# Attention weights times values in 64x64 pieces, and the scores of eight heads in one run

## The chip, the cores and the metric

The kernel runs on one core of a Trainium2 chip. The metric is the time of one execution on the device, in microseconds; the time of a version is the median of its runs. Below, PE is TensorE (its weight loads are counted apart, as PEld), DVE is VectorE, ACT is ScalarE, POOL is GpSimd and SP is SyncE, which issues nearly all transfers.

## What is computed

Four sequences of 768 positions, eight heads of 64 features. Attention with a distance bias, over a window of 96 keys back and 8 global keys, and then a channel mix on the result, in which each position is mixed with the one before it.

```python
keep = is_global | is_local          # pos < 8, or 0 <= rel < 96
bias = -slopes * dist
a = softmax(where(keep, q @ k.T / 8 + bias, -1e9))
x = (a @ v)                          # (4, 768, 512)
xk = mu_k * x + (1 - mu_k) * x_prev;  xr = mu_r * x + (1 - mu_r) * x_prev
k = maximum(xk @ w_k, 0)             # 512 -> 1024
out = sigmoid(xr @ w_r) * (k * k @ w_v)
```

All of it is float32. The products of the channel mix are made of three matmuls each on operands split into a high and a low part.

## The kernel before

**Tiles and steps.** The 3072 rows are 24 tiles of 128 queries, six to a sequence. A loop of 25 steps handles tile n's scores in step n (`scores`, `softmax`), and tile n-2's product with v in step n (`weighted`). A step has four parts, `hp` 0 to 3. Two tiles make a chunk of the channel mix (`ffn`, `channel_mix`), a generator of 40 pieces that the loop draws on after every part, 20 pieces a step; so two steps do one chunk: 16 pieces of `kp` (x times w_k, six matmuls of 256 columns each), 8 of `z` (three matmuls of 512 columns) and 16 of `vps` (three of 512). The mix runs about one step behind the x that it reads. One step of a pair therefore holds `kp` and `z` matmuls, the other the rest of `z`, all of `vps` and the beginning of the next `kp`.

**Tiles 6 and on** (`HEAD` = 6) take another way than the first six, and the change is in this way only.

- *Scores.* A key tile `kr` holds, for each half of 64 queries, the 8 global keys and the 160 before and in the half: 168 columns. Heads 0 to 3 lie in partitions 0 to 63 and heads 4 to 7 in 64 to 127, and each half of queries is a matmul of 64 rows (features) and 64 columns (queries) (L327). The first tile of a sequence (t = 0: tiles 6, 12 and 18) has no keys before it: 128 columns, one matmul of 64 rows and 128 columns a head. Four heads are scored in part 0 and four in part 2, into the two banks of `ps_s`.
- *Softmax.* For each head DVE adds the bias and takes the minimum (L369), ACT takes the exponential and its sum (L370), DVE the reciprocal of four sums (L381, L382), and POOL scales (L385).
- *Turning.* DVE transposes the weights in blocks of 32x32 (`turn`, L393 and L394), in part 2 for the first four heads and in part 0 of the next step for the other four. SP writes the blocks to DRAM (`send`, L404) and reads them back as 128 keys by 128 queries (`receive`, L416) into `landed`, which has two kinds of blocks: kind 0 for the keys of the tile before, kind 1 for the tile's own.
- *Product with v.* For each head two matmuls of 128 rows (keys) and 64 columns (features), over 128 queries: one on the v tile before, whose first 32 rows are overwritten with global keys (`global_v`, L280), one on the own v tile (L462). Queries that do not see a block of keys meet zeros in `landed`. Tiles with t = 0 have only the second. All heads go to the one bank of `ps_a`, and ACT copies it to x (L470).

**PSUM** has eight banks: two in `ps_s`, one in `ps_a`, five in `ps_f`, which turn around among `kp`, `z` and `vps` of the mix.

**What sets the order.** Each engine works its instructions off in the order in which they were built, and waits there for semaphores. The framework arranges that order by a timeline of its own, so the order on an engine is not that of the program text alone. A float32 matmul on unsplit operands stands once in the built order and twice in the trace.

The product with v, before:

```python
for u in range(2):
    o = s["av"][64 * u : 64 * u + 64, hp * 128 : (hp + 1) * 128]
    for k, vt in enumerate(blocks):
        c = 32 * (HH * (hp % 2) + 2 * (hp // 2) + u)
        g = landed[:, :, k + 2 - nb, c : c + 32]
        pe.matmul(o, vt[:, h * 64 : (h + 1) * 64], g, start=k == 0, stop=k == nb - 1)
```

## Time and profile before

| | |
|---|---|
| median of 3 runs | 479.29 us (478.5 to 482.03) |
| the profiled execution's own time | 479.75 us |
| its span, first to last instruction | 478.0 us |
| mean granted clock of TensorE | 0.989 |
| busy, share of the span | PE 97%, PEld 81%, DVE 65%, ACT 56%, POOL 39% |

Busy is the time in which an engine had at least one instruction in work. Matmuls are pipelined, so a busy PE may still do little per microsecond: what it does is read from the starts of its instructions.

### The profile page before, as it was taken

What the parts mean: (1) busy time and instruction counts of PE and PEld (TensorE: products, weight loads), DVE (VectorE), ACT (ScalarE), POOL (GpSimd) and SP (SyncE); (2) the same over time, 40 slices, a digit from 0 to 9 for tenths busy, and PEclk for the clock granted to TensorE, in tenths of its full rate; (3) what the DMA queues carried; (4) which work ended last, traced back from release to release, by engine and by line L of the source; (5) the groups of instructions that cost most, each with busy time, mean ns of one, the idle gap of its engine ahead of it and who ended that gap; (6) DMA issues with size and microseconds to landing.
All of it is one profiled execution on the core that took longest, in us unless ns stands there. A gap on an engine that the chain in (4) does not pass through costs nothing.

```text
span 478.0 us, 10000 instructions
## 1 busy us (share of the span) xinstructions
PE 463.4 (97%) x3506; PEld 386.1 (81%) x3506; DVE 311.0 (65%) x892; ACT 266.0 (56%) x644; POOL 188.0 (39%) x357
## 2 busy tenths in 40 slices
PE   7787999999999999999999999999999999999996
PEld 6666865688798898898797897897897897898985
DVE  6788979996757757646567666666567666546221
ACT  5876654536747648547548467466549458343220
POOL 7555687733423514414225415414315325303000
PEclk9987999999999999999999999999999999999999
DMA  5998530314476575567476575477476556140001
GB/s 174 290 262 287 175 149 27 78 62 110 128 192 159 170 190 156 167 185 195 120 188 164 156 216 148 126 196 197 99 200 163 155 165 159 51 135 22 23 2 49
DMA packets 64376, 70.37 MB, mean 147 GB/s; under 512 B 8032, under 2 KB 51296, under 8 KB 64320
## 3 DMA queue, kind: packets, MB, share of 16 engines
q1 hardware_dynamic: 64176, 69.66, 53.1%
q8 instruction: 30, 0.49, 0.5%
q14 instruction: 26, 0.21, 0.1%
q10 hardware_dynamic: 144, 0.00, 0.0%
HBM read 48.99 MB, written 19.66 MB: 144 GB/s over the span
## 4 chain that ended last, share of the span: by engine, by line
PE 77%; DVE 7%; POOL 1%; issue 0%; ACT 0%; DVEq 0%; ACTq 0%
PE vps L502 9%; PE kp L502 9%; PE vps L503 9%; PE vps L504 8%; PE kp L504 8%; PE kp L503 8%; PE av L462 7%; PE s L327 5%; PE z L502 5%; PE z L503 4%; PE z L504 4%; DVE wv_lo L193 1%; DVE wk_lo L193 1%; POOL wv_hi L218 1%; DVE room L369 1%; DVE wr_lo L193 1%
## 5 line engine op out<-in xcount | busy, mean ns | idle before, releaser
L385 POOL TENSOR_SCALAR room<-room,r 128x168 f32<-128x168 f32 (+2 forms) x160 | 79.7, 516 | 161.0 <-ACT kk L539 93.2
L370 ACT ACTIVATE room<-room,nmax 128x168 f32<-128x168 f32 (+2 forms) x192 | 83.3, 435 | 44.7 <-DVE nmax L369 44.6
L502 PE MATMUL kp<-xk_hi,wk_hi 128*128 128x256 f32 x352 | 101.0, 287 | 0.7 <-DVE kk L543 0.7
L504 PE MATMUL kp<-xk_hi,wk_lo 128*128 128x256 f32 x352 | 98.7, 280 | 0.0
L503 PE MATMUL kp<-xk_lo,wk_hi 128*128 128x256 f32 x352 | 98.4, 280 | 0.0
L502 PE MATMUL vps<-wv_hi,kk_hi 128*128 128x512 f32 (+1 forms) x184 | 72.1, 392 | 0.0
L503 PE MATMUL vps<-wv_lo,kk_hi 128*128 128x512 f32 (+1 forms) x184 | 71.2, 387 | 0.0
L502 PEld LDWEIGHTS kp<-xk_hi,wk_hi 128*128 128x128 f32 x352 | 66.9, 190 | 5.3 <-issue 3.3
L504 PE MATMUL vps<-wv_hi,kk_lo 128*128 128x512 f32 (+1 forms) x184 | 70.6, 384 | 0.0
L503 PEld LDWEIGHTS kp<-xk_lo,wk_hi 128*128 128x128 f32 x352 | 66.0, 188 | 0.7 <-DVE nmax L369 0.2
L504 PEld LDWEIGHTS kp<-xk_hi,wk_lo 128*128 128x128 f32 x352 | 66.1, 188 | 0.0
L544 ACT CAST kk_hi<-kk 128x512 fp32r<-128x512 f32 x44 | 27.3, 620 | 49.5 <-DVE kk L543 49.5
L545 DVE TENSOR_TENSOR kk_lo<-kk,kk_hi 128x512 fp32r<-128x512 f32 x44 | 31.4, 713 | 21.2 <-ACT kk_hi L544 21.2
L480 DVE SCALAR_TENSOR_TENSOR mix_k<-x,mus,mix_k 128x256 f32<-128x256 f32 x44 | 27.5, 663 | 25.9 <-POOL mix_k L479 25.9
L502 PEld LDWEIGHTS vps<-wv_hi,kk_hi 128*128 128x128 f32 x184 | 34.6, 188 | 9.6 <-issue 2.1
L479 POOL TENSOR_SCALAR mix_k<-x,mus 128x256 f32<-128x256 f32 x44 | 22.9, 538 | 45.8 <-ACT x L470 45.8
L504 PEld LDWEIGHTS vps<-wv_hi,kk_lo 128*128 128x128 f32 x184 | 34.5, 188 | 7.8
L503 PEld LDWEIGHTS vps<-wv_lo,kk_hi 128*128 128x128 f32 x184 | 34.6, 188 | 6.8
L462 PE MATMUL av<-room,va 128*64 128x128 f32 x608 | 39.3, 277 | 0.0
L539 ACT ACTIVATE kk<-kp 128x512 f32<-128x512 f32 x48 | 28.2, 587 | 17.6 <-PE kp L504 13.6
L462 PEld LDWEIGHTS av<-room,va 128*64 128x64 f32 x608 | 33.9, 136 | 5.0 <-issue 2.6
L543 DVE TENSOR_TENSOR kk<-kp,kk 128x512 f32<-128x512 f32 x44 | 30.0, 683 | 11.2 <-ACT kk L539 9.4
(119 smaller groups left out, 884.7 us busy)
## 6 DMA issues: line engine op xcount, KB each, us to landing
moved<-room SPq DMA_DIRECT2D x60, 192.0 KB
k<-in_k_rows_dram SPq DMA_DIRECT2D x60, 160.0 KB
room<-moved SPq DMA_DIRECT2D x30, 256.0 KB
out_dram<-sig SPq DMA_DIRECT2D x23, 256.0 KB
va<-in_v_dram SPq DMA_DIRECT2D x21, 256.0 KB
q<-in_qT_dram SPq DMA_DIRECT2D x36, 128.0 KB
w<-in_w_k_dram SPq DMA_DIRECT2D x8, 512.0 KB
w<-in_w_v_dram SPq DMA_DIRECT2D x8, 512.0 KB
```

The costliest lines, as they stand in the source:

```text
L327: pe.matmul(ps[i][q, u * 256 : u * 256 + w], s["qr"][o : o + 64, h, q], keys, start=True, stop=True)
L370: act.activation(e[:, :w], e[:, :w], AF.Exp, bias=s["nmax"][:, h : h + 1], scale=-1.0, accum_out=s["sum"][:, h : h + 1])
L385: pool.tensor_scalar(e[:, :w], e[:, :w], r[:, i : i + 1], 1.0, op0=ALU.mult, op1=ALU.mult)
L462: pe.matmul(o, vt[:, h * 64 : (h + 1) * 64], g, start=k == 0, stop=k == nb - 1)
L480: vec.scalar_tensor_tensor(tmp[:, j, :], xc[:, j, :], m[:, j : j + 1], tmp[:, j, :], op0=ALU.mult, op1=ALU.add)
L502: pe.matmul(o, sh, mh, start=first, stop=False)
L503: pe.matmul(o, sh, ml, start=False, stop=False)
L504: pe.matmul(o, sl, mh, start=False, stop=last)
L539: act.activation(kk, pv, AF.Relu)
L543: vec.tensor_mul(kk, pv, kk)
L544: act.copy(kkh[:, 2 * fp : 2 * fp + 2, :], kk)
L545: vec.tensor_sub(kkl[:, 2 * fp : 2 * fp + 2, :], kk, kkh[:, 2 * fp : 2 * fp + 2, :])
```

## The change

The product with v of tiles 6 and on is cut into pieces of 64 keys by 64 features. Rows 0 to 63 of the keys go to the old bank (`av`), rows 64 to 127 to a second one, taken from `ps_f` (`av2`); after ACT's copy of `av` to x, DVE adds `av2` to it (L483 of the changed kernel). The blocks in `landed` are laid out anew, so that of the two kinds of key blocks one is seen by all 128 queries and the other by 64 of them: per head and half of rows there is one matmul over 128 queries and one over 64. The keys before the tile come from a tile of their own, `vb` (96 rows of v and the 32 global rows), which SP loads into `room[:, 7]` for each tile with t > 0; before, only the 32 rows were written into the old v tile.

All eight heads of a tile are scored in part 0, the first four into two banks of `ps_f`, the other four into `ps_s`. `turn` follows in parts 2 and 3 of the same step, `send` in part 3, and `receive` in part 0 of the next step.

```diff
--- before.py
+++ after.py
@@ -277,7 +277,9 @@
         b, t = divmod(n, NT)
         if n >= HEAD:
             if t:
-                nc.sync.dma_start(state[n - 1]["va"][0:32], vg)
+                vb = state[n]["vb"] = room[:, 7]
+                nc.sync.dma_start(vb[0:BACK], v[b, t * 128 - BACK : t * 128])
+                nc.sync.dma_start(vb[BACK:128], vg)
                 return
             for hh in range(HH):
                 heads = slice(HH * (hh // 2) + hh % 2, HH * (hh // 2) + hh % 2 + 3, 2)
@@ -315,9 +317,9 @@
             p = patw if t else pat0
         if n >= HEAD:
             ps = {}
-            for j in (hp // 2,):
+            for j in range(2):
                 for i in (j, j + 2):
-                    ps[i] = ps_s.tile([128, 512], F32, name=f"s_{n}_{i}", tag="s")
+                    ps[i] = (ps_s if j else ps_f).tile([128, 512], F32, name=f"s_{n}_{i}", tag="s" if j else "f")
                 for u in range(2):
                     h = 2 * j + u
                     for half in (0, 1) if t else (None,):
@@ -325,7 +327,7 @@
                         for o, i in ((0, j), (64, j + 2)):
                             keys = s["kr"][o : o + 64, h, 1, WIN - 128 : WIN] if half is None else s["kr"][o : o + 64, h, half]
                             pe.matmul(ps[i][q, u * 256 : u * 256 + w], s["qr"][o : o + 64, h, q], keys, start=True, stop=True)
-            rounds = [(j, [(i, ps[i]) for i in (j, j + 2)])]
+            rounds = [(j, [(i, ps[i]) for i in (j, j + 2)]) for j in range(2)]
         elif n < PADDED:
             ps = ps_s.tile([128, 512], F32, name=f"s_{n}_{hp}", tag="s")
             for u in range(2):
@@ -390,26 +392,23 @@
         e = room[:, 8 + 2 * j : 10 + 2 * j].rearrange("p a (u x) -> p (a u) x", u=2)
         out = turned[:, :, 128 * j : 128 * j + 128].rearrange("p l (h i) -> p h l i", h=HH)
         if n % NT:
-            vec.transpose(out[:, :, 0], e[:, :, 0:GMAX].rearrange("p (r h) k -> p r h k", r=1).to_broadcast([128, 4, HH, GMAX]))
-            vec.transpose(out[:, :, 1:6], e[:, :, GMAX:WIN].rearrange("p h (l c) -> p h l c", l=5))
-        else:
-            vec.transpose(out[:, :, 2:6], e[:, :, 0:128].rearrange("p h (l c) -> p h l c", l=4))
+            vec.transpose(out[:, :, 5], e[:, :, 0:GMAX].rearrange("p (r h) k -> p r h k", r=1).to_broadcast([128, 4, HH, GMAX]))
+            vec.transpose(out[:, :, 0:5], e[:, :, GMAX:WIN].rearrange("p h (l c) -> p h l c", l=5))
+        else:
+            vec.transpose(out[:, :, 0:4], e[:, :, 0:128].rearrange("p h (l c) -> p h l c", l=4))
 
     def send(n):
         if n < HEAD:
             return
-        l0 = 0 if n % NT else 2
+        nl = 6 if n % NT else 4
         moved = state[n]["moved"] = d_pool.tile([4, 6, 32, 256], F32, name=f"moved_{n}", tag="moved")
         for a in range(4):
-            nc.sync.dma_start(moved[a].rearrange("l q x -> q l x")[:, l0:6], turned[32 * a : 32 * a + 32, l0:6])
+            nc.sync.dma_start(moved[a].rearrange("l q x -> q l x")[:, 0:nl], turned[32 * a : 32 * a + 32, 0:nl])
 
     def receive(n):
         if n < HEAD:
             return
         moved = state[n].pop("moved")
-        if n == HEAD:
-            pool.memset(landed[:, 2:4, 0], 0.0)
-            pool.memset(landed[:, 0:2, 1], 0.0)
 
         def land(a, l, k, p):
             src = moved[a, l].rearrange("a l q x -> (l q) a x")
@@ -417,13 +416,13 @@
 
         A, B = slice(0, 2), slice(2, 4)
         if n % NT:
-            land(A, slice(0, 4), 0, 0)
-            land(B, slice(0, 1), 0, 0)
-            land(B, slice(1, 2), 0, 96)
-            land(A, slice(4, 6), 1, 0)
-            land(B, slice(2, 6), 1, 0)
-        else:
-            land(slice(0, 4), slice(2, 6), 1, 0)
+            land(A, slice(0, 3), 0, 0)
+            land(B, slice(0, 1), 0, 64)
+            land(slice(0, 4), slice(5, 6), 0, 96)
+            land(A, slice(3, 5), 1, 0)
+            land(B, slice(1, 5), 1, 0)
+        else:
+            land(slice(0, 4), slice(0, 4), 1, 0)
 
     def transposes(n, hp):
         if n >= HEAD:
@@ -445,21 +444,32 @@
         s = state[n]
         if hp == 0:
             s["av"] = ps_a.tile([128, 512], F32, name=f"av_{n}", tag="av")
-        blocks = [state[n - 1]["va"], s["va"]] if t else [s["va"]]
-        nb = len(blocks)
+            if n >= HEAD:
+                s["av2"] = ps_f.tile([128, 512], F32, name=f"av2_{n}", tag="f")
         if n < HEAD:
+            blocks = [state[n - 1]["va"], s["va"]] if t else [s["va"]]
+            nb = len(blocks)
             et = s.pop(("et", hp))
-        for u in range(2):
-            h = 2 * hp + u
-            o = s["av"][64 * u : 64 * u + 64, hp * 128 : (hp + 1) * 128]
-            for k, vt in enumerate(blocks):
-                if n < HEAD:
+            for u in range(2):
+                h = 2 * hp + u
+                o = s["av"][64 * u : 64 * u + 64, hp * 128 : (hp + 1) * 128]
+                for k, vt in enumerate(blocks):
                     c = (u * nb + k) * 128
-                    g = et[:, c : c + 128]
-                else:
+                    pe.matmul(o, vt[:, h * 64 : (h + 1) * 64], et[:, c : c + 128], start=k == 0, stop=k == nb - 1)
+        else:
+            lo, hi = slice(0, 64), slice(64, 128)
+            every, own, back = slice(0, 4), 1, 0
+            first, second = [("va", own, every), ("vb", back, slice(0, 2))], [("vb", back, every), ("va", own, slice(2, 4))]
+            if not t:
+                first = second = [("va", own, every)]
+            for k in range(len(first)):
+                for u in range(2):
+                    h = 2 * hp + u
                     c = 32 * (HH * (hp % 2) + 2 * (hp // 2) + u)
-                    g = landed[:, :, k + 2 - nb, c : c + 32]
-                pe.matmul(o, vt[:, h * 64 : (h + 1) * 64], g, start=k == 0, stop=k == nb - 1)
+                    for rows, bank, parts in ((lo, "av", first), (hi, "av2", second)):
+                        vt, kind, a = parts[k]
+                        o = s[bank][64 * u : 64 * u + 64, hp * 128 + 32 * a.start : hp * 128 + 32 * a.stop]
+                        pe.matmul(o, s[vt][rows, h * 64 : h * 64 + 64], landed[rows, a, kind, c : c + 32], start=k == 0, stop=k == len(first) - 1)
         if hp == 3:
             c, i = divmod(n, 2)
             if i == 0:
@@ -467,7 +477,10 @@
                     pool.memset(xt[:, :, 0:1], 0.0)
                 else:
                     pool_copy(xt[:, :, 0:1], xt[:, :, 256:257])
-            act.copy(xt[:, :, 1 + 128 * i : 129 + 128 * i], s["av"].rearrange("p (a q) -> p a q", a=4))
+            x = xt[:, :, 1 + 128 * i : 129 + 128 * i]
+            act.copy(x, s["av"].rearrange("p (a q) -> p a q", a=4))
+            if n >= HEAD:
+                vec.tensor_add(x, s["av2"].rearrange("p (a q) -> p a q", a=4), x)
 
 
     def mix(xc, xp, tag, tmp_pool, out_pool):
@@ -615,16 +628,15 @@
                 global_v(step - 1)
             if step:
                 if hp == 0:
-                    turn(step - 1, 1)
-                    send(step - 1)
-                if hp == 1:
                     receive(step - 1)
                 transposes(step - 1, hp)
             if step < NTILES:
-                if step < HEAD or hp % 2 == 0:
+                if step < HEAD or hp == 0:
                     scores(step, hp)
-                if hp == 2:
-                    turn(step, 0)
+                if hp > 1:
+                    turn(step, hp - 2)
+                if hp == 3:
+                    send(step)
             if hp == 0:
                 if step >= LAG and (step - LAG) % 2 == 0:
                     queue.append(ffn((step - LAG) // 2))
```

What the change does to the order is shown at three places. All are in the step of tile 17's scores, one that holds `z` and `vps` work of the mix. `s_17_i` are the score banks of tile 17, `av_15` and `av2_15` the product of tile 15, `va_15` its v tile, `room` the tile with the weights and `vb`.

PE at the product of tile 15, before: the first five rows, all 128 rows by 64 columns over 128 queries, on the two v tiles in turn (16 such rows in all).

```order
L462 MATMUL av_15_3428<-room_205,va_14_2784 64x128
L462 MATMUL av_15_3428<-room_205,va_15_3001 64x128
L462 MATMUL av_15_3428<-room_205,va_14_2784 64x128
L462 MATMUL av_15_3428<-room_205,va_15_3001 64x128
L462 MATMUL av_15_3428<-room_205,va_14_2784 64x128
```

The same place now, the first eight of 32 rows.

```order
L472 MATMUL av_15_3587<-room_205,va_15_3122 64x128
L472 MATMUL av2_15_3588<-room_205 64x128
L472 MATMUL av_15_3587<-room_205,va_15_3122 64x128
L472 MATMUL av2_15_3588<-room_205 64x128
L472 MATMUL av_15_3587<-room_205 64x64
L472 MATMUL av2_15_3588<-room_205,va_15_3122 64x64
L472 MATMUL av_15_3587<-room_205 64x64
L472 MATMUL av2_15_3588<-room_205,va_15_3122 64x64
```

Each row of before has become two, on two banks, and every second pair of rows goes over 64 queries in place of 128.

PE at the scores that follow, before: the end of the product, four heads (banks 0 and 2), then the mix.

```order
L462 MATMUL av_15_3428<-room_205,va_14_2784 64x128
L462 MATMUL av_15_3428<-room_205,va_15_3001 64x128
L327 MATMUL s_17_0_3454<-k_17_3333,q_17_3332 64x168
L327 MATMUL s_17_2_3455<-k_17_3333,q_17_3332 64x168
L327 MATMUL s_17_0_3454<-k_17_3333,q_17_3332 64x168
L327 MATMUL s_17_2_3455<-k_17_3333,q_17_3332 64x168
L327 MATMUL s_17_0_3454<-k_17_3333,q_17_3332 64x168
L327 MATMUL s_17_2_3455<-k_17_3333,q_17_3332 64x168
L327 MATMUL s_17_0_3454<-k_17_3333,q_17_3332 64x168
L327 MATMUL s_17_2_3455<-k_17_3333,q_17_3332 64x168
L502 MATMUL z_3419<-wr_hi_67,xr_hi_3068 128x512
L503 MATMUL z_3419<-wr_lo_10_1053,xr_hi_3068 128x512
```

The same place now: the end of banks 0 and 2 (seven more rows of these two stand ahead), all of banks 1 and 3, then the mix.

```order
L329 MATMUL s_17_2_3631<-k_17_3510,q_17_3509 64x168
L329 MATMUL s_17_1_3640<-k_17_3510,q_17_3509 64x168
L329 MATMUL s_17_3_3641<-k_17_3510,q_17_3509 64x168
L329 MATMUL s_17_1_3640<-k_17_3510,q_17_3509 64x168
L329 MATMUL s_17_3_3641<-k_17_3510,q_17_3509 64x168
L329 MATMUL s_17_1_3640<-k_17_3510,q_17_3509 64x168
L329 MATMUL s_17_3_3641<-k_17_3510,q_17_3509 64x168
L329 MATMUL s_17_1_3640<-k_17_3510,q_17_3509 64x168
L329 MATMUL s_17_3_3641<-k_17_3510,q_17_3509 64x168
L515 MATMUL z_3578<-wr_hi_67,xr_hi_3231 128x512
L516 MATMUL z_3578<-wr_lo_10_1053,xr_hi_3231 128x512
```

Before, the rows of `s_17_1` and `s_17_3` stood 30 rows further down, between the two halves of `vps`; they now follow at once, and no score row interrupts the mix any more.

DVE in the same step, before, around the low part of the next chunk's input (`xk_lo`, `xr_lo`): the transposes of four heads and a product of `sig` with `vps` follow it.

```order
L381 TENSOR_SCALAR r_17_0_0_3472<-sum_17_3341 128x4
L480 SCALAR_TENSOR_TENSOR mix_r_3492<-x_206,mus_63,mix_r_3492 128x256 x2
L382 RECIPROCAL r_17_0_0_3472<-r_17_0_0_3472 128x4
L482 TENSOR_TENSOR xk_lo_3481<-mix_k_3479,xk_hi_3480 128x1024
L482 TENSOR_TENSOR xr_lo_3494<-mix_r_3492,xr_hi_3493 128x1024
L393 STREAM_TRANSPOSE room_205<-room_205 128x128
L394 STREAM_TRANSPOSE room_205<-room_205 128x4x5x32
L571 TENSOR_TENSOR sig_3418<-vps_3514,sig_3418 128x512
L369 ISA room_205,nmax_17_3342<-s_17_1_3554,patw_845 128x168
```

The same place now.

```order
L493 SCALAR_TENSOR_TENSOR mix_r_3693<-x_206,mus_63,mix_r_3693 128x256 x2
L384 RECIPROCAL r_17_0_0_3658<-r_17_0_0_3658 128x4
L495 TENSOR_TENSOR xk_lo_3682<-mix_k_3680,xk_hi_3681 128x1024
L383 TENSOR_SCALAR r_17_0_1_3673<-sum_17_3518 128x4
L495 TENSOR_TENSOR xr_lo_3695<-mix_r_3693,xr_hi_3694 128x1024
L384 RECIPROCAL r_17_0_1_3673<-r_17_0_1_3673 128x4
L395 STREAM_TRANSPOSE room_205<-room_205 128x128
L396 STREAM_TRANSPOSE room_205<-room_205 128x4x5x32
L395 STREAM_TRANSPOSE room_205<-room_205 128x128
L396 STREAM_TRANSPOSE room_205<-room_205 128x4x5x32
L584 TENSOR_TENSOR sig_3577<-vps_3715,sig_3577 128x512
L584 TENSOR_TENSOR sig_3712<-vps_3754,sig_3712 128x512
```

The reductions of `s_17_1` and `s_17_3` have moved ahead of `xk_lo`. Behind `xr_lo` now stand both pairs of transposes, and only then the two `sig` products, which read the `vps` banks; the addition of `av2_16` is behind these. The scores of the next tile take the bank of the first of the two `vps`: `s_18_2` waits for DVE there.

## Rows read from the trace of the kernel before

**Rows 1.** the page, part 1: busy time, share of the span, instructions
```profile
PE 463.4 (97%) x3506; PEld 386.1 (81%) x3506; DVE 311.0 (65%) x892; ACT 266.0 (56%) x644; POOL 188.0 (39%) x357
```

**Rows 2.** windows: stretch, its length, busy PE, PEld, DVE, ACT, POOL; clock, DMA share, GB/s
```profile
254.65:290.35 35.70, 35.70 (x297) 30.34 (x296) 24.41 (x71) 22.22 (x51) 13.24 (x27) 1.00 0.61 164
```

**Rows 3.** waits of PE, whole span: waiting <- waited for: total us, times, longest
```profile
PE t L439 <- POOL room L385: 6.5, 5, 3.2
...
PE s L335 <- issue: 0.3, 1, 0.3
```

**Rows 4.** timeline of PE: start us, us, engine line operation out<-in xcount
```profile
254.09 0.40 PE L503 MATMUL z<-wr_lo,xr_hi 128*128 128x512 f32 x1
254.32 0.40 PE L504 MATMUL z<-wr_hi,xr_lo 128*128 128x512 f32 x1
254.65 2.02 PE L462 MATMUL av<-room,va 128*64 128x128 f32 x32
256.60 0.80 PE L327 MATMUL s<-k,q 64*64 64x168 f32 x16
257.33 0.50 PE L502 MATMUL z<-wr_hi,xr_hi 128*128 128x512 f32 x1
257.67 0.40 PE L503 MATMUL z<-wr_lo,xr_hi 128*128 128x512 f32 x1
...
264.20 0.40 PE L504 MATMUL vps<-wv_hi,kk_lo 128*128 128x512 f32 x1
264.53 0.80 PE L327 MATMUL s<-k,q 64*64 64x168 f32 x16
265.26 0.50 PE L502 MATMUL vps<-wv_hi,kk_hi 128*128 128x512 f32 x1
265.60 0.39 PE L503 MATMUL vps<-wv_lo,kk_hi 128*128 128x512 f32 x1
...
272.46 2.02 PE L462 MATMUL av<-room,va 128*64 128x128 f32 x32
```

**Rows 5.** groups of TensorE by line and shape: count | busy us, mean ns | idle
```profile
L462 PE MATMUL av<-room,va 128*64 128x128 f32 x608 | 39.3, 277 | 0.0
L327 PE MATMUL s<-k,q 64*64 64x168 f32 x480 | 24.0, 315 | 0.0
L327 PEld LDWEIGHTS s<-k,q 64*64 64x64 f32 x480 | 14.8, 132 | 6.7 <-issue 5.9
L502 PEld LDWEIGHTS z<-wr_hi,xr_hi 128*128 128x128 f32 x88 | 16.6, 188 | 5.3 <-issue 2.3
```

**Rows 6.** timeline of DVE
```profile
258.59 0.32 DVE L369 CUSTOM_DVE_ANT_0 room<-s,patw 128x168 f32<-128x168 f32 x1
258.84 0.32 DVE L369 CUSTOM_DVE_ANT_0 room<-s,patw 128x168 f32<-128x168 f32 x1
...
273.02 0.31 DVE L393 STREAM_TRANSPOSE room<-room 128x128 f32<-128x128 f32 x1 [1.74 <-POOL room L385]
273.25 0.80 DVE L394 STREAM_TRANSPOSE room<-room 128x640 f32<-128x640 f32 x1
```

**Rows 7.** timeline of POOL
```profile
271.44 1.54 POOL L385 TENSOR_SCALAR room<-room,r 128x168 f32<-128x168 f32 x4 [4.09 <-DVE r L382]
```

**Rows 8.** groups of DVE and POOL by line and shape
```profile
L480 DVE SCALAR_TENSOR_TENSOR mix_k<-x,mus,mix_k 128x256 f32<-128x256 f32 x44 | 27.5, 663 | 25.9 <-POOL mix_k L479 25.9
L482 DVE TENSOR_TENSOR xr_lo<-mix_r,xr_hi 128x1024 fp32r<-128x1024 f32 x11 | 14.3, 1296 | 0.4 <-ACT xr_hi L481 0.4
L571 DVE TENSOR_TENSOR sig<-vps,sig 128x512 f32<-128x512 f32 x23 | 15.2, 659 | 11.8 <-PE vps L504 11.8
L480 DVE SCALAR_TENSOR_TENSOR mix_r<-x,mus,mix_r 128x256 f32<-128x256 f32 x44 | 22.6, 554 | 0.0
L482 DVE TENSOR_TENSOR xk_lo<-mix_k,xk_hi 128x1024 fp32r<-128x1024 f32 x11 | 13.5, 1223 | 6.1 <-ACT xk_hi L481 6.1
L479 POOL TENSOR_SCALAR mix_r<-x,mus 128x256 f32<-128x256 f32 x44 | 25.7, 600 | 0.0
```

## The prediction

> **What bounds the kernel now.** I read the page first: PE is busy for 97% of the span, DVE for 65% [rows 1]. A busy PE need not be a bound, so next the windows: over two steps in the middle, 35.70 us, PE is busy for all 35.70, at the full clock, DVE for 24.41, with transfers at 0.61 of their engines [rows 2]. The list of PE's waits has six rows, from 6.5 to 0.3 us, and its largest is on a line of the first six tiles [rows 3]. So PE sets the time from about tile 6 on, and what counts is how long its blocks take, start to start. The reader is to see in the timeline how a block of attention stands among the matmuls of the mix [rows 4].
>
> **What a block costs now.** Matmuls of `z` start 0.23 us apart (254.09, 254.32). The block of product and four heads' scores lies between the starts 254.32 and 257.67: 3.35, less two spacings, 2.89 us. The second four heads lie between 264.20 and 265.60: 1.40 less 0.46, 0.94 us. A step pays 3.83 us for both [rows 4].
>
> What is in these? The product: 32 matmuls in 2.02 us, each 0.277 long [rows 4, 5], so a pair of them takes (2.02 - 0.28)/16 = 0.109 us, 0.85 ns for each of 128 queries. The scores: if four pieces run at once at that same rate, a round over 168 keys takes 0.143, and four rounds 3 x 0.143 + 0.315 (the mean of one [rows 5]) + about 0.05 for the first weights = 0.80. The row says 0.80; at two pieces at once it would be some 1.35. So pieces of 64x64 run four at a time, each at the speed of a wider one. This is the ground of the forecast.
>
> The rest is fixed cost. Four rounds are 0.57, so an interruption of the mix costs 0.94 - 0.57 = 0.37. The first block holds one such, 16 pairs (1.74), four rounds (0.57), and 2.89 - 0.37 - 1.74 - 0.57 = 0.21 between product and scores, where the shape goes from 128*64 to 64*64.
>
> **The change part by part, on PE.**
>
> 1. *Product in quarters.* For two heads there are now two rounds over 128 queries and two over 64 (two passes each, four quarters at once): 4 x (2 x 0.109 + 2 x 0.055) = 1.31 in place of 1.74. Saved: 0.43 for each of 15 tiles with t > 0. Rounds over 64 queries are not in the trace. From below they cost 0.055, by the column; a load of 64 columns takes 0.188 - 0.132 = 0.056 longer for twice that width [rows 5], so the weights of the next round just fit behind. From above they cost 0.109, like the round over 128. I take 0.055, since the scores keep to the rate per column; the other end is 0.43 x 15 = 6.5 us dearer. Tiles with t = 0 have eight rounds over 128, as before: nothing saved.
> 2. *Eight heads in one go.* One interruption less: 0.37.
> 3. *Product and scores of one shape.* The 0.21 between them goes, where the scores too are 64*64. If not, 0.21 x 14 = 2.9 us are lost again.
>
> Sum: eleven steps with both kinds of t > 0 save 0.43 + 0.37 + 0.21 = 1.01, 11.1 us; two whose scores are of a first tile 0.80, 1.6; three whose product is of a first tile 0.58, 1.7; the last two tiles, with no scores behind, 0.43, 0.9; steps 6 and 7, with an old product, 0.37, 0.7. Together 16.0 us.
>
> **What must stay hidden.** DVE gets 18 additions of 128x512 out of PSUM; the nearest row takes 0.659 [rows 8], so 1.3 us more in two steps, where it rests 11 of 35.7 [rows 2]. SP gets 192 KB more for each of 15 tiles, some 7% on the 164 GB/s of two steps [rows 2]; each is asked for a whole step before its use. Both are taken as nothing. The banks are the risk: the five of `ps_f` now also hold two scores and `av2`, so PE waits for DVE at places where it did not. I follow DVE through the step of the order shown, from the first product matmul of tile 15 (time 0). Product out at 1.6; ACT's copy (0.66 by the nearest row) 2.3; the addition 2.9; POOL's first mix product (0.60) 3.5. Then DVE does eight mix products (4 x 0.663 + 4 x 0.554 = 4.9), eight reductions 0.25 apart (2.0), `xk_lo` (1.22) and two tiny ones: 11.9 [rows 6, 8]. PE wants `xk_lo` after 1.4 + 8 x 0.143 + 0.37 + 54 x 0.23 = 15.3, so 3.4 us to spare. On: `xr_lo` (1.30) and the reciprocal 13.4; a pair of transposes (0.23 + 0.80) 14.4; the second pair after POOL's four products (1.54 from 13.4 [rows 7]) 14.9 to 16.0; the first `sig` 16.6 [rows 6, 8]. PE wants that bank for `s_18_2` at the next step's scores. A step was 272.46 - 254.65 = 17.81 [rows 4], now 16.8, so at 16.8 + 1.4 = 18.2: 1.6 us to spare. In the other step of the pair DVE has no mix to make. The transposes are done earlier than before, so `send` and `receive` gain time. So no wait comes up by these rows, but the room is small.
>
> **Sum.** 479.75 - 16.0 = 463.75 for the profiled execution, which stood 0.46 above the median of the runs: **463.3 us**.
>
> **Rivals.**
>
> *Banks come late* (chance 0.07). If DVE's chain is 3 us longer than I made it, say through mix products and transposes that each wait a little for POOL, PE waits 1.4 us once in two steps, eight times: 11 us, 475. For it: DVE works strictly in order and now waits for POOL in that chain twice. Against it: 1.6 us to spare with the longer mean for half the mix products.
>
> *Weight loads show* (0.04). If a quarter could not take its next weights while its matmul runs, each of 16 rounds would cost 0.056 more, 0.90 a product, and the gain of a usual step shrinks to 0.11; over all steps some 2 us would be left, 478. Against it: the scores' 0.80 leaves room for one load, not for four [rows 4]. [...]
>
> *PE cannot be fed so fast* (0.05), the one with the other sign. A usual block now has 96 matmuls in 2.45 us, 0.026 each, in place of 48 in 2.44, 0.051. It breaks even at (3.83 - 0.37)/96 = 0.036. The scores alone show 16 in 0.49, 0.031 each, but a short run may come out of a stock. If no long run can go denser than the 0.051 seen, a block costs 96 x 0.051 + 0.37 = 5.27, 1.44 more than before, in 13 steps 19 us: 498. Against it: after the scores the mix starts on its regular spacing, with no sign of a stock run dry. [...]
>
> **How the numbers follow.** My forecast, with the bounds of its unknown costs (463 to 473 with both the dear rounds and the shape change), has 0.80; the rivals 0.16; 0.04 is left for what I do not see. The range of 8 in 10 is 460 to 471: below, for the waits of the first 100 us, which may shrink or grow as the order moves; above, up to the dear rounds. One per cent, 4.8 us, is about what a measurement of this kernel can tell from no change. Below 474.5 lie the forecast, half of the late banks and some of the rest: faster 0.86. Same: the other half and the weight loads, 0.08. Slower 0.06.
>
> **What would show it.** Right: in the timeline of PE a product of 64 matmuls in about 1.6 us, with no gap to 32 scores in about 1.4; no score between two matmuls of `vps`; steps of 16.8 us; PE's list of waits as short as before. Wrong: waits of PE for DVE at `s`, `kp` or `z` (banks); starts of product rounds 0.1 us or more apart where 64 queries are streamed (rounds or loads); matmuls spread evenly at 0.04 us or more through the block (feeding).

## The result, and the profile after

The changed kernel takes **463.94 us** (median of 4 runs, 461.75 to 468.04) against 479.2 (478.5 to 482.03): ratio 0.970, 95% interval 0.962 to 0.978. The forecast was 463.3 with a range of 460 to 471. The profiled execution took 461.75; forecast for it were 463.75.

The page, part 1 (busy time, share of the span of 459.6 us, instructions), the answer to [rows 1]:

```profile
PE 446.5 (97%) x4034; PEld 379.5 (83%) x4034; DVE 314.9 (69%) x910; ACT 267.2 (58%) x644; POOL 184.4 (40%) x355
```

TensorE has 528 matmuls more than before and is busy for 17 us less. Its waits over the whole span, the answer to [rows 3] (waiting, waited for, us in total, times, longest):

```profile
PE t L438 <- POOL room L387: 4.1, 5, 2.8
PE kp L515 <- DVE nmax L371: 1.3, 1, 1.3
PE idle L88 <- DVE zeros L85: 1.1, 1, 1.1
PE s L338 <- POOL pat L142: 0.9, 1, 0.9
PE vps L577 <- DVE word L181: 0.5, 1, 0.5
PE s L337 <- POOL pat L142: 0.3, 1, 0.3
```

All six lie in the first 110 us. Now the same two steps as in [rows 2] (columns as there):

```profile
245.10:278.86 33.76, 33.76 (x361) 29.61 (x360) 22.80 (x70) 21.11 (x51) 12.16 (x26) 1.00 0.74 197
```

33.76 us in place of 35.70, TensorE busy throughout and at the full clock. VectorE rests 11.0 us of them (11.3 before), and the transfers take 0.74 of their engines' time against 0.61 (in the pair of steps behind it 0.69 against 0.67). The block of a usual step, in the timeline of TensorE, the answer to [rows 4]:

```profile
244.58 0.40 PE L516 MATMUL z<-wr_lo,xr_hi 128*128 128x512 f32 x1
244.82 0.40 PE L517 MATMUL z<-wr_hi,xr_lo 128*128 128x512 f32 x1
245.15 0.32 PE L472 MATMUL av<-room,va 64*64 64x128 f32 x1
245.15 0.32 PE L472 MATMUL av<-room 64*64 64x128 f32 x1
245.16 0.32 PE L472 MATMUL av<-room,va 64*64 64x128 f32 x1
245.17 0.32 PE L472 MATMUL av<-room 64*64 64x128 f32 x1
245.31 0.27 PE L472 MATMUL av<-room,va 64*64 64x128 f32 x1
...
245.42 0.22 PE L472 MATMUL av<-room,va 64*64 64x64 f32 x1
...
245.47 0.22 PE L472 MATMUL av<-room 64*64 64x64 f32 x1
...
246.54 1.32 PE L329 MATMUL s<-k,q 64*64 64x168 f32 x32
247.79 0.50 PE L515 MATMUL z<-wr_hi,xr_hi 128*128 128x512 f32 x1
248.13 0.40 PE L516 MATMUL z<-wr_lo,xr_hi 128*128 128x512 f32 x1
```

Read it by starts. Four matmuls begin within 0.02 us (245.15 to 245.17): the four pieces of 64x64 of one round. Once in its rhythm a round over 128 queries lasts 0.11 (245.31 to 245.42) and one over 64 lasts 0.05 (245.42 to 245.47). The product begins at 245.15, the scores at 246.54 without a gap, and the mix is back at 247.79. From 244.82 to 248.13 are 3.31 us; less two spacings of the mix, the block costs **2.84** where the two blocks of before cost 3.83 by the rows and 3.81 by the unrounded starts.

Below, "block" always means this: from the start of the last mix matmul ahead to the start of the second one behind, less the spacings of these two, from starts in ns. The **stretch** is the time from the last mix matmul ahead of step 7's block to the end of the span; it leaves out the first 110 us.

| block, us | before (both goes) | after | saved | forecast |
|---|---|---|---|---|
| usual step (11 of them) | 3.81 | 2.84 | 0.97 | 1.01 |
| scores of a first tile (2) | 3.63 | 2.79 | 0.84 | 0.80 |
| product of a first tile (3) | 2.89 | 2.37 | 0.52 | 0.58 |
| product alone, last steps (2) | 2.15 | 1.69 | 0.45 | 0.43 |
| step 7, old product (1) | 3.81 | 3.45 | 0.36 | 0.37 |

These 19 steps save 15.2 us; the stretch fell from 364.4 to 349.5, by 14.9. What is ahead of it began its last matmul at 113.59 before and at 110.16 now: 3.4 us, of which step 6 was to give 0.37 and no step of the change the rest (see the first experiment).

### The profile page after: what moved, and what is told of

Read it like the earlier page. It is cut to its first block, busy times and chain, and to the rows that moved or that the text cites. A ratio compares the mean times of both kernels' runs of the same rounds, so it can differ in the third digit from the quotient of the medians.

```text
span 459.6 us, 11121 instructions
## 1 busy us (share of the span) xinstructions
PE 446.5 (97%) x4034; PEld 379.5 (83%) x4034; DVE 314.9 (69%) x910; ACT 267.2 (58%) x644; POOL 184.4 (40%) x355
## 4 chain that ended last, share of the span: by engine, by line
PE 77%; DVE 6%; POOL 1%; issue 0%; ACT 0%; DVEq 0%; ACTq 0%
PE kp L515 9%; PE vps L516 9%; PE vps L515 9%; PE vps L517 9%; PE kp L517 9%; PE kp L516 9%; PE av L472 6%; PE z L515 5%; PE z L516 4%; PE z L517 4%; PE s L329 4%; DVE wv_lo L193 1%; DVE wk_lo L193 1%; POOL wv_hi L218 1%; DVE wr_lo L193 1%; DVE room L371 1%
## 5 line engine op out<-in xcount | busy, mean ns | idle before, releaser
L387 POOL TENSOR_SCALAR room<-room,r 128x168 f32<-128x168 f32 (+2 forms) x160 | 76.9, 498 | 78.0 <-DVE r L384 67.4
L515 PE MATMUL vps<-wv_hi,kk_hi 128*128 128x512 f32 (+1 forms) x184 | 71.1, 387 | 0.0
L492 POOL TENSOR_SCALAR mix_k<-x,mus 128x256 f32<-128x256 f32 x44 | 24.4, 572 | 116.2 <-DVE x L483 99.1
L481 ACT COPY x<-av 128x512 f32<-128x512 f32 x24 | 14.0, 585 | 61.4 <-PE av L472 59.7
L483 DVE TENSOR_TENSOR x<-av,x 128x512 f32<-128x512 f32 x18 | 12.5, 692 | 47.1 <-ACT x L481 47.1
L558 DVE TENSOR_TENSOR kk_lo<-kk,kk_hi 128x512 fp32r<-128x512 f32 x44 | 29.4, 683 | 14.3 <-ACT kk_hi L557 13.7
L372 ACT ACTIVATION_READ_ACCUMULATOR room<-room,nmax 128x1 f32 x192 | 36.1, 188 | 0.0
```

The costliest lines, as they stand in the source:

```text
L372: act.activation(e[:, :w], e[:, :w], AF.Exp, bias=s["nmax"][:, h : h + 1], scale=-1.0, accum_out=s["sum"][:, h : h + 1])
L387: pool.tensor_scalar(e[:, :w], e[:, :w], r[:, i : i + 1], 1.0, op0=ALU.mult, op1=ALU.mult)
L492: pool.tensor_scalar(tmp[:, j, :], xp[:, j, :], m1[:, j : j + 1], 1.0, op0=ALU.mult, op1=ALU.mult)
L515: pe.matmul(o, sh, mh, start=first, stop=False)
L558: vec.tensor_sub(kkl[:, 2 * fp : 2 * fp + 2, :], kk, kkh[:, 2 * fp : 2 * fp + 2, :])
```

## The experiments

In the table, "step 7" is where the stretch begins in the run's profiled execution. The kernel before ran on the same chips at 475.7 to 476.6 us in the median.

| kernel | time, us | step 7 | stretch | usual block |
|---|---|---|---|---|
| changed kernel | 463.94 | 110.16 | 349.5 | 2.84 |
| x0_after | 464.81 | 115.26 | 349.4 | 2.84 |
| x1_two_goes | 468.80 | 110.44 | 355.8 | 2.27 + 0.93 |
| x2_old_product | 471.68 | 109.86 | 358.3 | 3.45 |
| x3_full_rounds | 470.12 | 112.16 | 355.4 | 3.25 |
| x7_no_add | 463.20 | 112.55 | 349.3 | 2.84 |
| x8_first_square | 468.00 | 116.59 | 348.8 | 2.84 |
| x4_rounds_of_64 | 463.19 | 111.41 | 351.1 | 2.90 to 2.92 |
| x5_rounds_of_32 | 504.16 | 111.83 | 390.4 | 4.30 to 6.29 |
| x10_weights_of_32 | 471.39 | 113.42 | 357.5 | 3.32, once 3.59 |
| x6_four_banks | 470.97 | 117.03 | 350.1 | 2.84 |
| x9_copies_4 | 476.04 | 113.31 | 360.4 | 2.84, or cut in three |
| x9_copies_6 | 476.36 | 110.66 | 362.8 | 2.84, or cut in three |

### The changed kernel once more

> The changed kernel itself, beside the others on the same chip. Both theories: 462 to 466 us, ratio to the kernel before 0.966 to 0.973; usual block of product and eight heads' scores 2.84 us between the matmuls of the mix. If the time of the first 110 us is what varies from run to run, the steps from 127 us on last 16.80 and 16.96 us again and any difference to 461.75 lies ahead of them.

464.81 us (462.62 to 466.59), ratio 0.973 (0.969 to 0.978). Beside the kernel before on the same chip (476.62) this is 11.8 us less, where the first comparison gave 15.3 and the stretch alone 14.9. So the part ahead of the stretch lost some 3 us, an estimate from medians; the kernel before was profiled once only, so where it lost them stays open.

The stretch is the same to 0.1 us, but it begins 5.1 us later. The same window of the changed kernel, and then of this run (columns as in [rows 2]; the clock is third from the end):

```profile
20.00:40.00 20.00, 15.88 (x113) 12.29 (x112) 19.89 (x63) 17.09 (x49) 12.61 (x17) 0.93 1.04 279
```

```profile
20.00:40.00 20.00, 14.35 (x95) 11.35 (x94) 15.96 (x51) 15.09 (x44) 11.07 (x16) 0.80 1.03 260
```

In both, the transfer engines are busy all through 20 to 40 us (shares of 1.04 and 1.03). In the first TensorE does 113 matmuls there at a mean granted clock of 0.93, in the second 95 at 0.80. Taken matmul by matmul, the second profile isn't behind at 22 us and is 5.2 us behind at 43. So the difference of these two profiles arises where weights of the mix are loaded. The stretch is the part in which small effects can be read from one profile, and it is what the experiments below are read by.

### Four heads in each of two goes

```diff
-            for j in range(2):
+            for j in (hp // 2,):
...
-                if step < HEAD or hp == 0:
+                if step < HEAD or hp % 2 == 0:
                     scores(step, hp)
```

(with turn, send and receive where they were before, and all scores in the two banks of `ps_s` again)

> The new product, but the scores in two goes again, four heads in part 0 and four in part 2, with the turning, sending and receiving in their old places. Theory (an interruption of the mix costs 0.37 us, whatever stands in it): the block of a usual step becomes 0.37 + 1.31 + 0.57 = 2.25, the second four heads 0.94, together 3.19 in place of 2.84; 18 steps by 0.36 is 6.5 us, 468 in place of 462. Rival (the gain is all in the product, the interruption costs only what its rounds last): second go 0.57, the sum stays 2.84, 462.

468.80 us (ratio 0.984, 0.980 to 0.988). The usual block became 2.27 and the second go 0.93, 3.20 where 3.19 was expected; the stretch grew by 6.3 us (6.5 expected, with step 6, which lies ahead of the stretch); 0.45 of it is the last product alone, 2.15 in place of 1.69, for which the profile shows no wait. The second go, in the timeline of this kernel:

```profile
257.22 0.40 PE L517 MATMUL vps<-wv_hi,kk_lo 128*128 128x512 f32 x1
257.55 0.80 PE L329 MATMUL s<-k,q 64*64 64x168 f32 x16
258.28 0.50 PE L515 MATMUL vps<-wv_hi,kk_hi 128*128 128x512 f32 x1
```

Between two mix matmuls that otherwise start 0.23 apart lies 1.06 (257.22 to 258.28), for four rounds of 0.143. (The block of 0.93 also counts the slower second mix matmul, which starts 0.33 after the first and not 0.23.) The rival, that the interruption costs only its rounds, is out.

### The old product with the new scores

The product, its layout and its bank are those of before; eight heads are scored in part 0.

> Eight heads in one go, but the old product: pieces of 128 keys by 64 features, one bank, the old layout of the turned weights. Theory (rounds by the column, 0.21 for the change of shape between product and scores): usual block 0.37 + 1.74 + 0.21 + 1.14 = 3.46, 0.62 more than 2.84 in 11 steps; 0.43 in the two whose scores are of a first tile, 0.2 in the three whose product is, 0.45 in the last two: 9.2 us in all, 471 in place of 462. Rival (the gain is all in the missing interruption, quarters are no faster): 462 to 463.

471.68 us (ratio 0.989, 0.986 to 0.993); stretch 8.8 us longer (9.2 expected), usual block 3.45 (3.46 expected), with a first tile's product 2.52, with a first tile's scores 3.24, product alone 2.15. The block in this kernel's timeline:

```profile
247.69 0.40 PE L504 MATMUL z<-wr_hi,xr_lo 128*128 128x512 f32 x1
248.02 2.02 PE L462 MATMUL av<-room,va 128*64 128x128 f32 x32
249.97 1.37 PE L327 MATMUL s<-k,q 64*64 64x168 f32 x32
251.27 0.50 PE L502 MATMUL z<-wr_hi,xr_hi 128*128 128x512 f32 x1
```

From product to scores are 1.95 (248.02 to 249.97), as in [rows 4]. Take the interruption (0.37), 16 pairs (1.74) and eight rounds (1.14) from 3.45: 0.20 is left for the change of shape. The two halves of the change undone apart, 6.3 and 8.8, make 15.1, where together they saved 14.9: they add up, within the 0.45 above.

### Quarters without the cut of the queries

```diff
-            first, second = [("va", own, every), ("vb", back, slice(0, 2))], [("vb", back, every), ("va", own, slice(2, 4))]
+            first, second = [("va", own, every), ("vb", back, every)], [("vb", back, every), ("va", own, every)]
```

> The changed kernel, but the pieces over 64 queries go over all 128 again (the halves that do not see the keys meet zeros). It tells the cut of the queries from the cut into quarters. Theory (a round costs 0.85 ns for each query, so quarters by themselves save nothing, and all of the product's gain is in the queries left out): product 1.31 to 1.74, usual block 3.27, 15 tiles by 0.43 is 6.5 us, 468 in place of 462. Rival (rounds over 64 cost what rounds over 128 cost, and quarters are faster by themselves): block 2.84, 462.

470.12 us (ratio 0.987, 0.983 to 0.990); usual block 3.25 (3.27 expected), product alone 2.10 in place of 1.69, stretch 5.9 us longer (6.5 expected). The product alone in this kernel's timeline, from the last mix matmul ahead to the second one behind:

```profile
403.59 0.28 PE L520 MATMUL kp<-xk_hi,wk_lo 128*128 128x256 f32 x1
...
405.71 0.38 PE L518 MATMUL kp<-xk_hi,wk_hi 128*128 128x256 f32 x1
405.93 0.28 PE L519 MATMUL kp<-xk_lo,wk_hi 128*128 128x256 f32 x1
```

These are 2.34, less two spacings 2.10; the old product alone cost 2.15. So the rounds of 64x64 pieces are no faster in themselves; what is left of the usual block's gain, 3.45 to 3.25, goes with the change of shape, which isn't there in this kernel either. The product's own gain is all in the queries left out, and these could be left out only because the keys were cut in halves.

### The addition left out

> The changed kernel without VectorE's addition of the second bank to x, so x lacks half of the keys' part. Theory (the 18 additions, 0.69 us each, lie beside TensorE's work): the stretch from step 7's block to the end stays at 349.4 us (it was 349.5 and 349.4 in the two traces of the changed kernel), 462 to 466 us in all. Rival (VectorE's chain sets when the next chunk can start): 0.7 to 1.4 us less in each pair of steps, 6 to 11 us less, 451 to 458.

463.20 us; the stretch is 349.3, with the additions 349.4 and 349.5: here they cost nothing.

### A first tile's scores as squares

```diff
-                    for half in (0, 1) if t else (None,):
-                        q = slice(0, 128) if half is None else slice(64 * half, 64 * half + 64)
+                    for half in (0, 1):
+                        q = slice(64 * half, 64 * half + 64)
                         for o, i in ((0, j), (64, j + 2)):
```

> The changed kernel with the scores of a first tile of a sequence in pieces of 64 by 64 like all others (two half pieces over the same 128 keys in place of one of 64 by 128; the same columns at four pieces at once). Theory (0.21 us is the price of changing the shape between product and scores): the block of steps 12 and 18 goes from 2.79 to 2.58, all others stay at 2.84 and 2.37; 0.4 us in all, not to be seen in the time, 462 to 466. Rival (the 0.21 belongs to the product or to the length of the block): 2.79 stays.

The block of steps 12 and 18 is 2.57 in place of 2.79, all others are unchanged. So a change of shape between product and scores costs 0.22 here, with the same columns on both sides; the rival, which leaves 2.79, is out. Whether it is the shape itself or the load of weights 128 columns wide, the run doesn't tell. The stretch is 0.6 us shorter than that of the changed kernel; the time, 468.0, shows it no more, since step 7 began at 116.59 in its profile.

### Shorter rounds of the same columns

```diff
-            first, second = [("va", own, every), ("vb", back, slice(0, 2))], [("vb", back, every), ("va", own, slice(2, 4))]
+            first = [("va", own, p, 1, 0), ("vb", back, p, 0, 1), ("va", own, q, 1, 1)]
+            second = [("vb", back, p, 1, 1), ("vb", back, q, 1, 0), ("va", own, q, 0, 1)]
```

(p and q are the halves of the queries; the numbers open and close a sum. For 32 the same with quarters of the queries.)

> The changed kernel with the product in three rounds over 64 queries per pair of heads and pass, in place of one over 128 and one over 64: the same columns, half as many matmuls again (96 instead of 64 a tile), each with weights of its own. Theory (a round costs its columns, weight loads of 0.056 just fit behind 0.055): product 24 x 0.055 = 1.32, usual block 2.84 as before, 462 to 466 us. Rival A (weight loads show where they are as long as the matmul): 24 x (0.055 + 0.056) = 2.66, block 4.2, 1.35 x 15 = 20 us more. Rival B (matmuls cannot be fed denser than the 0.021 us of the product now): 96 x 0.021 = 2.0, block 3.5, 10 us more.

> The changed kernel with the product in six rounds over 32 queries: the same columns again, 192 matmuls a tile, each half as long as the load of its weights. Theory (the load of 64 columns, some 0.056 us by the rows, sets the pace once the matmul is shorter): 48 x 0.056 = 2.7 in place of 1.32, usual block 4.2, 15 x 1.37 = 21 us more, 483 to 487. Rival A (loads of other quarters hide it still, by the column alone): 2.84, 462 to 466. Rival B (feeding at 0.021 a matmul): 192 x 0.021 = 4.0, block 5.5, 40 us more, 503.

With rounds over 64 the product alone costs 1.754 in place of 1.695, and 24 rounds are (1.754 - 0.37)/24 = 0.0577 each, not 0.055. The blocks of a first tile's product rose more than this, by 0.20 to 0.23; the cause stays open. The stretch is 1.6 us longer. With rounds over 32 two things happen, and my theory had only the first. The cleanest product alone costs 3.126: 48 rounds of (3.126 - 0.37)/48 = 0.0574, the same as over 64, for half the columns. That is near the 0.056 expected, and it makes 1.46 x 15, 22 us; with some 3 us in the first tiles' products 25 of the 41 us by which the stretch grew. Of the other 16, 10.9 are the second thing. The waits of TensorE in this kernel:

```profile
PE av L474 <- issue: 8.5, 7, 2.0
...
PE s L329 <- issue: 2.4, 3, 1.1
```

And its timeline in one such place:

```profile
149.34 0.32 PE L474 MATMUL av<-room 64*64 64x32 f32 x3
151.36 0.26 PE L474 MATMUL av<-room 64*64 64x32 f32 x3 [1.70 <-issue]
```

After 154 of the product's 192 matmuls, the engine stands still for nearly 2 us and waits for nothing that the profile shows. The usual blocks that come from `z` all have such a stall (5.29 to 6.29), the three that come from `kp` have none (4.30). This is as the forecast's rival "PE cannot be fed so fast" has it, though no row shows the cause: it came after 154 matmuls at 0.015 us each, where the changed kernel has 64 at 0.021. The time, 504.16, is nearly that of rival B (503), but by chance: B has all 192 matmuls 0.021 apart, and here they come 0.015 apart with single stalls.

### Narrower weights

```diff
-                        o = s[bank][64 * u : 64 * u + 64, hp * 128 + 32 * a.start : hp * 128 + 32 * a.stop]
-                        pe.matmul(o, s[vt][rows, h * 64 : h * 64 + 64], ...)
+                        for d in (0, 32):
+                            o = s[bank][64 * u + d : 64 * u + d + 32, hp * 128 + 32 * a.start : hp * 128 + 32 * a.stop]
+                            pe.matmul(o, s[vt][rows, h * 64 + d : h * 64 + d + 32], ...)
```

> The changed kernel with each piece of the product cut across the features: two pieces of 64 keys by 32 features in place of one of 64 by 64, over the same queries. 128 matmuls a tile in place of 64, none shorter, each with weights half as wide. It asks what set the pace of rounds over 32 queries (0.0575 us for four). Theory A (the load of 64 columns of weights; pieces of 64 by 32 run eight at once): 1.32 us as now, usual block 2.84. Theory B (matmuls with their loads come at 0.0144 us each at best): 128 x 0.0144 = 1.84, block 3.36, 8 us more in 15 tiles. Theory C (four at once is all there is, whatever their width): 2.64, block 4.16, 20 us more.

The stretch grew by 8.0 us, as B has it, and the usual block to 3.32 (once 3.59); but the product alone costs 2.01, of which 1.64 are rounds, between A (1.32) and B (1.84). The timeline of one product in this kernel shows why:

```profile
407.10 0.30 PE L473 MATMUL av<-room,va 64*32 64x128 f32 x2
407.11 0.30 PE L473 MATMUL av<-room 64*32 64x128 f32 x2
407.13 0.30 PE L473 MATMUL av<-room,va 64*32 64x128 f32 x2
407.14 0.30 PE L473 MATMUL av<-room 64*32 64x128 f32 x2
407.23 0.28 PE L473 MATMUL av<-room,va 64*32 64x128 f32 x2
...
407.55 0.29 PE L473 MATMUL av<-room 64*32 64x128 f32 x1
407.56 0.27 PE L473 MATMUL av<-room,va 64*32 64x128 f32 x1
```

Eight begin within 0.05 us (407.10 to 407.14), then nothing until 407.23: eight at once, at the pace of A. So C is out. From 407.54 on they come one by one: the last 95 matmuls start 0.0131 us apart on average. What sets this pace, and why it does not hold for the first 33, no row shows. With scores behind it the block loses more (0.48) than the product alone (0.32), but not at that pace: by the starts 0.11 more lie between the last product matmul and the first score (0.146 in place of 0.039) and 0.05 in the first round of scores, and the other rounds start 0.143 apart as before. A change of shape from 64x32 to 64x64 would fit; it wasn't tested. The 0.0131 is faster than the 0.0144 that B took from the run with rounds over 32 as the least for a matmul with its load. The load of 64 columns, 0.056 by the forecast's estimate, is near the 0.0574 for a round of four there, and the starts in that run, four 6.5 ns apart and then a pause, fit it too. But the two paces lie too close to call it shown.

### One bank less

```diff
-    ps_f = fast.enter_context(tc.tile_pool(name="ps_f", bufs=5, space=PSUM))
+    ps_f = fast.enter_context(tc.tile_pool(name="ps_f", bufs=4, space=PSUM))
```

> The changed kernel with four banks in place of five for the mix, av2 and two scores; one bank lies unused. Theory (the room before the scores is 1.4 us, one user of a bank less and it is gone): waits of TensorE for VectorE at s, kp, z or vps of 1 to 3 us in each pair of steps, 8 to 25 us in all, 472 to 490. Rival (banks are no concern; the fifth is never needed in time): no such waits, 462 to 466.

The theory fell. TensorE's list has one wait on a bank, and it stands at 99 us, in step 6:

```profile
PE s L329 <- DVE sig L584: 2.2, 1, 2.2
```

From step 7 on the stretch is 350.1, 0.6 us longer than with five banks, all of it in the three blocks with a first tile's product (2.51 to 2.72 in place of 2.37). The 470.97 us of the whole come from ahead of it: step 7 began at 117.03, later than in any other run here; this wait makes 2.2 us of it.

### A longer chain on VectorE

```diff
                 vec.tensor_add(x, s["av2"].rearrange("p (a q) -> p a q", a=4), x)
+                for again in range(4):
+                    vec.tensor_copy(x, x)
```

> The changed kernel with four copies of x to itself on VectorE right behind the addition, some 0.65 us each by the row of xr_lo, 2.6 us more a step. In the order, sig and one pair of transposes have moved ahead of xk_lo, so xk_lo comes 2.6 + 0.65 + 1.03 = 4.3 us later, against 3.9 us of room in the trace of the changed kernel (xk_lo done at 290.1, its first reader on TensorE at 294.0). Theory (room of 3.9 us for xk_lo and 1.4 us for the bank of the scores, else nothing): 0 to 0.4 us of wait in each pair, 349.4 becomes 349 to 353. Rival (VectorE's chain is already on the path): all of 2.6 us once in a pair of steps, 21 us more.

> The same with six copies, 3.9 us more a step. In the order only half of mix_r stands ahead of xk_lo, so it comes 3.9 + 0.65 + 1.03 - 1.1 = 4.5 us later, and xr_lo and the scores' bank follow. Theory (room 3.9 us): 0.6 us of wait in each pair, 349.4 becomes 353 to 358. Rival (chain already on the path): 3.9 us once in a pair, 31 us more. Rival B (the order gives way, VectorE has 9 us of rest in a pair of steps, nothing shows): 349 to 350.

476.04 and 476.36 us; the stretch grew by 11.0 and 13.4, more than the theory's 0 to 3 and 4 to 9, less than the rival's 21 and 31. A copy took 0.425 us, less than I had taken. The waits are where they were expected, on `xk_lo`; in the kernel with four copies

```profile
PE kp L518 <- DVE xk_lo L497: 3.3, 7, 1.3
```

is 0.47 us each (with six copies 4.3 us, 0.61 each). That this is near the size expected is luck. By the expectation's own sum the copies as they were, 4 x 0.425 = 1.7 us, make `xk_lo` 1.7 + 0.65 + 1.03 = 3.4 us later, inside the room, and no wait. But the order on VectorE had changed further. In the timeline of VectorE in this kernel, for the product that starts at 253.02:

```profile
263.37 0.27 DVE L383 TENSOR_SCALAR r<-sum 128x4 f32<-128x4 f32 x1 [2.55 <-ACT room L372]
...
268.61 1.21 DVE L497 TENSOR_TENSOR xk_lo<-mix_k,xk_hi 128x1024 fp32r<-128x1024 f32 x1
```

`xk_lo` is done 16.8 us after the product's start, in place of 11.2, and VectorE rests 2.55 us for ScalarE in the midst of the chain.

The larger part is on the other engine, and the expectation left it out: the framework, with its own idea of when things are ready, also took the product apart. The timeline of TensorE in the kernel with four copies:

```profile
268.14 0.40 PE L519 MATMUL vps<-wv_hi,kk_lo 128*128 128x512 f32 x1
268.46 0.43 PE L472 MATMUL av<-room,va 64*64 64x128 f32 x2
268.82 0.39 PE L517 MATMUL kp<-xk_hi,wk_hi 128*128 128x256 f32 x1
269.14 0.32 PE L472 MATMUL av<-room 64*64 64x128 f32 x1
...
269.87 0.39 PE L518 MATMUL kp<-xk_lo,wk_hi 128*128 128x256 f32 x1 [0.19 <-DVE xk_lo L497]
...
271.36 0.27 PE L472 MATMUL av<-room 64*64 64x64 f32 x1
```

Two product matmuls, one of `kp`, ten of the product, more of `kp`, then the rest: three interruptions in place of one. The three pieces of this step cost 0.45 + 1.04 + 2.61 = 4.10, 1.26 more than the whole block, of which the wait is 0.19. The seven steps cut like this cost 11.0 us more in all, the whole growth of the stretch; 3.3 of it are the waits.

## Why the prediction was right, step by step

**Bound.** TensorE alone set the time from step 7 on, and it still does: in the two steps shown it is busy for all 33.76 us, and none of its waits is later than 110 us.

**Rounds by the column** (0.43 a tile, with 0.055 taken for 64 queries and 0.109 as the dear end). Right: 1.31 was forecast for the product and (1.69 - 0.37) = 1.32 came. Full rounds cost 0.41 a tile, and the stretch gives 5.9 of the 6.5 us that were at stake. The reading behind it, that the 0.80 of 16 score pieces allows only four at once at the pace of one, carried the forecast.

**The interruption** (0.37). Right: two goes cost 0.36 more a step. This came from one subtraction, 0.94 less four rounds, and the product alone (2.15 less 16 pairs, 0.40) was within 0.03 of it.

**The change of shape** (0.21). Right in size, 0.20 with the old product and 0.22 for the first tiles' scores, and right that it goes where both are 64x64. In one place it was taken too large: behind a first tile's old product the run gives only 2.52 - 2.37 = 0.15, which is why 0.52 and not 0.58 was saved there.

**The sum.** 15.7 us were forecast for the steps from 7 on, and the blocks gave 15.2. The usual step's 1.01 was 0.97, since 3.83 and the pieces that I took it apart into were read from starts rounded to 0.01 us. The 0.3 by which the stretch fell less than the blocks isn't placed.

**The first 110 us** were forecast as unchanged. The same kernel began step 7 at 110.16 and 115.26. And by the medians on the same chip they grew by some 3 us (14.9 saved in the stretch, 11.8 in the time). The forecast started from runs of the kernel before that were slower than its later ones: from 476.62 it would have been 476.62 - 16.0 = 460.6, where 464.81 came. So the agreement of the medians to 0.6 us is luck; what the runs bear out is the stretch.

**What must stay hidden.** The chain on VectorE went as followed through the order. The product of tile 15 starts at about 278.9, and in the changed kernel's timeline of VectorE and of TensorE stand:

```profile
288.93 1.19 DVE L495 TENSOR_TENSOR xk_lo<-mix_k,xk_hi 128x1024 fp32r<-128x1024 f32 x1
...
295.02 1.25 DVE L584 TENSOR_TENSOR sig<-vps,sig 128x512 f32<-128x512 f32 x2
```

```profile
294.37 0.28 PE L516 MATMUL kp<-xk_lo,wk_hi 128*128 128x256 f32 x1
...
297.25 1.16 PE L329 MATMUL s<-k,q 64*128 64x128 f32 x16
```

`xk_lo` is done at 290.1, 11.2 us after the product's start (forecast 11.9), 4.2 before TensorE reads it (forecast 3.4). The first `sig` is done at about 295.65, 1.6 us before the scores that take its bank, and 1.6 was forecast. "The room is small" was too dark, though: with a bank less the framework placed the work otherwise, and the wait came up only once, ahead of the stretch. What the runs with copies show to be dear is to be late with x.

**The rivals.** *Banks late* did not come. *Weight loads show* did not come in the changed kernel: its rounds over 64 queries keep to their columns, 0.05 each (245.42 to 245.47). Where all rounds went over 64, 24 of them, each piece with a load of its own, took 0.0577 us each; by the forecast's estimates a round alone takes 0.055, and round and load in turn would take 0.11. *PE cannot be fed so fast* had its breaking point at 0.036 us a matmul. The changed kernel's product runs at 1.32/64 = 0.021, and stalls or slower rounds showed only at 0.013 to 0.015.

## What to carry to other kernels

Where one engine is busy throughout, price its blocks from start to start and split them into a rate and a fixed part; here a rate by the column, 0.37 us for each interruption of the mix and 0.2 us for each change of tile shape gave the gain of the stretch to within half a microsecond. Cut into pieces of 64x64 over the same columns, the product was hardly faster here (2.10 against 2.15 us alone); it gained where the smaller pieces let columns be left out (1.69), and no more where the pieces were shorter still (a round over 32 queries took 0.0574 us, one over 64 0.0577, and over 32 the engine stood still for 10.9 us in all). And when work is added on a side engine under such a framework, read the order of the main engine too: with four copies the waits cost 3.3 us, and the rearranged product the rest of 11.0.

## What the runs showed of the hardware

- Pieces of 64 by 32 ran eight at once: in the run with narrower weights eight began within 0.05 us (407.10 to 407.14), and a round of eight over 128 queries lasted 0.11, as a round of four pieces of 64 by 64 did in the changed kernel (245.31 to 245.42). This held for the first 32 of a product's 128 matmuls.
- In products that stand alone, a round of four pieces, each with its own 64 columns of weights, took 0.0577 us over 64 queries and 0.0574 over 32 (the block less 0.37, through 24 and 48 rounds).
- The ten stalls in the run with rounds over 32, 10.9 us in all and the longest 2.0, have no releaser in the profile; they stand there as `issue`. Beside them the pages of the changed kernel and of this run differ in the row of one queue (packets, MB, share):

```profile
q8 instruction: 34, 0.56, 0.6%
```

```profile
q8 instruction: 51, 0.84, 0.7%
```

These are 17 packets more, with 4416 more weight loads and matmuls in the trace (2 x (6242 - 4034)). Around the stall shown above, the window from 146 to 149.44 us holds one packet of this queue, that from 149.44 to 151.4 none. Whether TensorE waited for such a packet no row shows.
